# One bank rotation for scores and gradients in the attention core of a fused backward kernel

## The chip, the core and the metric

The kernel runs on one core of a Trainium2 chip. The metric is the device time of one execution in microseconds (us). A core has five engines with a queue of instructions each: TensorE (PE, matrix products, into PSUM banks), VectorE (DVE), ScalarE (ACT), GpSimd (POOL) and SyncE (SP, which here issues transfers). They wait for each other on semaphores, and each runs its own queue in order.

## The reference

Two attention blocks, A and B, read inputs of 2048 tokens with 448 features; the forward output and the gradients of all eight inputs are computed. Block A is linear attention and is untouched here. Block B has 16 heads of width 28 that share one key and one value head:

```
q = (x @ wq) per head;  k = x @ wk;  v = x @ wv
p = softmax(q k^T * 28 ** -0.5);  o = p v;  out = concat(o) @ wo
_out, _vjp = jax.vjp(forward, all inputs);  grads = _vjp(grad_out)
```

Its backward pass needs, for every pair of query and key, the exponential of the score, and the gradient of the probability (the row of "do" against v, less a row term) multiplied with it.

## The kernel before, in words

A prologue computes block A with its gradients and the projections of block B. Then comes the core, one loop over `u`. The queries are cut into 64 blocks `b` (256 query tokens of two heads), and each block into eight steps of 256 keys: `u = 8 b + tp`, 512 steps. The scores of step `u` and the gradients of step `w = u - 16` are computed in one pass of the loop, so that gradients run two blocks behind scores. The order of every engine's queue is the order of the program text (`tc.manual_schedule`).

Eight PSUM banks of 512 words for 128 partitions are in use: three in `SB` (named aacc in the profile), two in `DB` (agen), `oq` and `dk_acc` (agen), and `dv_acc` (aacc). One pass of the loop does, in this order:

- `rows_SD` (its matmuls have the line of `mmt`, L664): eight matmuls of 256 columns, two halves for each of four results: the scores of two heads (sp[0], sp[1]) and the gradients of two heads (dp[0], dp[1]). The tuple (k, h) in `todo` means score (k=0) or gradient (k=1) of head h. The list gives their order in TensorE's queue.
- In even steps `o_dq`, the products for o and dq into `oq`. Then, each once in eight steps and always in even steps, work that uses a bank called `spare`: `onat_T` at u mod 8 = 2, `don_T` at 6, `out_proj` or `do_proj` at 0.
- ScalarE: exponential of sp[0] into `eT` (L935); copy of dp[1] into `cp` (L951); at the end of the pass exponential of sp[1] (L983).
- VectorE: `dst[0] = dp[0] * eT[0]` (L949). POOL: `dst[1] = cp * eT[1]` (L952).
- VectorE's small work, each piece once in eight steps: at u mod 8 = 1 a copy of `oq` (L965), at 2 `o_norm` (L808, L809, which read the spare bank), at 3 L968, at 4 `row_D` (L821, which reads no bank; POOL's L822 behind it), at 6 `don_copy` (L837, reads the spare), at 0 `out_store` (L736) or `do_copy` (L900), which read the spare.
- After the exponentials, each fourth step, SyncE issues a transposing transfer eT to eN.
- In odd steps 16 matmuls `dk_m` that read a transposed block `dsx`; in even steps `o_dq` again and, in three steps out of eight, `dv_mm`.
- In odd steps VectorE transposes the `dsT` pair of the two steps before the last into `dsx` (L1016).

In the kernel before, the scores use the three banks of `SB`, in an order that repeats every four steps, and the one left over is the spare. The gradients use the two banks of `DB`, always the same: dp[0] is DB[0] and dp[1] is DB[1].

Of the kernel before, what the change touches and what calls it, by code (L numbers as in the profile page):

```python
# [8 lines left out]
ACT = mybir.ActivationFunctionType  # L9
# [16 lines left out]
def kernel(  # L26
# [21 lines left out]
    nc = tc.nc  # L48
# [3 lines left out]
    scale = float(DH) ** -0.5  # L52
# [550 lines left out]
    def q_shift(pn, shift, tmp):  # L603
        a = tmp[0][0:H, :]
        nc.scalar.activation(out=a, in_=pn[0:H, :], func=ACT.Identity, bias=eps[:, 0:1], scale=kmax2[:, 0:1])
        i32 = mybir.dt.int32
        nc.vector.tensor_scalar(out=a.bitcast(i32), in0=a.bitcast(i32), scalar1=1, scalar2=None, op0=ALU.logical_shift_right)
        nc.vector.tensor_scalar(out=shift, in0=a, scalar1=1.004 * 2.0 ** 63.5, scalar2=None, op0=ALU.mult)
# [22 lines left out]
    with ExitStack() as cs_:  # L631
# [9 lines left out]
        SB = [psA.tile([P, 512], F32, name="aacc") for i in range(3)]  # L641
        DB = [psA.tile([P, 512], F32, name="agen") for i in range(2)]
        oq, dk_acc = (psA.tile([P, 512], F32, name="agen") for _ in range(2))

        dsT, dsx, qX, don, doT, rl, prod, pairs = ({} for _ in range(8))
        ETs = [pe_.tile([P, 4, 2, 512], BF16, name=f"eT{i}") for i in range(5)]
        ENs = [pn_.tile([P, 32, P], BF16, name=f"eN{i}") for i in range(5)]

        def eT(u):
            return ETs[u // 4 % 5][:, u % 4, :, :]  # L650
# [3 lines left out]
        def half():  # L654
            if not halves:
                t = pd_.tile([P, 2, 2, 512], BF16, name="dsT")
                halves.extend([t[:, 0, :, :], t[:, 1, :, :]])
            return halves.pop(0)
# [4 lines left out]
        def mmt(out, lhsT, rhs, pos, start, stop):  # L663
            nc.tensor.matmul(out, lhsT=lhsT, rhs=rhs, start=start, stop=stop, tile_position=pos,  # L664
                             skip_group_check=True)

        def blk(b):
            qc, pair = divmod(b, 8)
            return qc, pair, pair // 2, pair % 2

        def rows_SD(u, sp, dp):
            b, tp = divmod(u, 8)
            w = u - 16
            qc, pair, g, hp = blk(b)
            todo = [(0, 0), (0, 1), (1, 0), (1, 1)] * 2
            if sp is not None and dp is not None:
                todo = [(0, 0), (1, 0)] * 2 + [(0, 1), (1, 1)] * 2 if u % 2 else \
                    [(0, 0), (0, 1), (1, 0)] * 2 + [(1, 1)] * 2
            seen = {}
            for d in todo:  # L680
                if (dp if d[0] else sp) is None:
                    continue
                k, h = d
                t2 = seen.get(d, 0)
                seen[d] = 1
                t = 2 * tp + t2
                tc_ = slice(t * P, (t + 1) * P)
                oc = slice(t2 * 256, (t2 + 1) * 256)
                r = 64 * (1 - hp if k else hp) + 32 * h
                if k:  # L690
                    mmt(dp[h][:, oc], vT_rep[r:r + 32, tc_], doT[w // 8][r:r + 32, :], (r, 0), True, True)
                else:
                    mmt(sp[h][:, oc], kT_rep[r:r + 32, tc_], qT_B[g][r:r + 32, qc * 256:(qc + 1) * 256],
                        (r, 0), True, True)
# [149 lines left out]
        def qc_T(st, qc, g):  # L844
            nc.sync.dma_start_transpose(qX[qc].rearrange("p b s c -> p (b s) c")[:, :, g * P:(g + 1) * P],
                                        st.rearrange("p n a j -> p (n a j)"))
# [43 lines left out]
        def do_proj(i, c0, c1, ps):  # L890
            for c in range(4):
                if c1 - c0 == 512:
                    mm(ps[:, :], gbT[:, i, c, :], woTp[:, c, :], start=(c == 0), stop=(c == 3))
                    continue
                for j in range(4):
                    js = slice(32 * j, 32 * j + 32)
                    mmt(ps[js, 0:c1 - c0], gbT[:, i, c, js], woTp[:, c, c0:c1], (0, 32 * j), c == 0, c == 3)
# [6 lines left out]
        with tc.manual_schedule():  # L904
# [8 lines left out]
            for u in range(NU + 28):  # L913
                w = u - 16
                hasS = u < NU
                hasD = 0 <= w < NU
                b0, b1, spare = ((SB[i] for i in ((0, 1, 2), (0, 2, 1), (1, 0, 2), (1, 2, 0))[u % 4]) if hasS else SB)
                sp = [b0, b1] if hasS else None
                dp = DB if hasD else None
                rows_SD(u, sp, dp)  # L920
                if u % 2 == 0:
                    o_dq((u - 2,), (u - 20,))
# [5 lines left out]
                    out_proj(*op, spare)  # L928
                dpj = do_slots.pop(u, None)
                if dpj is not None:  # L930
                    dps_ = DB[u // 2 % 2] if u < 16 else dk_acc if u < 27 else spare
                    do_proj(*dpj, dps_)

                if hasS:
                    nc.scalar.activation(out=eT(u)[:, 0, :], in_=sp[0][:, :], func=ACT.Exp, scale=scale)  # L935
                if u == 1:
                    q_shift(pn3, shifts[3], [half().rearrange("p a b -> p (a b)").bitcast(F32)])
                    halves.clear()
                    dv_acc = psA.tile([P, 512], F32, name="aacc")
# [40 lines left out]
                if dpj is not None:  # L980
                    do_copy(*dpj, dps_)
                if hasS:
                    nc.scalar.activation(out=eT(u)[:, 1, :], in_=sp[1][:, :], func=ACT.Exp, scale=scale)  # L983
                    if u % 4 == 3:
                        nc.sync.dma_start_transpose(ENs[u // 4 % 5][:, :, :],
                                                    ETs[u // 4 % 5][:, :, :, :].rearrange("p a b c -> p (a b c)"))
                    if 0 <= gq < 4 and iq == 1 and u < 448:
                        qc_T(qst, qq, gq)

                if u % 2:  # L990
                    b, i = divmod(u - 27, 8)
# [20 lines left out]
                if 0 <= y < NU and y % 2:  # L1012
                    b, tp = divmod(y, 8)
                    if tp == 1:
                        dsx[b] = px_.tile([P, 8, 2, 2, 256], BF16, name="dsx")
                    nc.vector.transpose(  # L1016
                        out=dsx[b][:, tp - 1:tp + 1, :, :, :].rearrange("p u h t c -> p (u h t c)").bitcast(F32),
                        in_=pairs[y // 2].rearrange("p u h c -> p (u h c)").bitcast(F32))
# [70 lines left out]
        for c in range(4):  # L1089
            r = DC_ROWS[c]  # L1090
            ps = gen(0)
            for st in range(NS):
# [3 lines left out]
                                 func=ACT.Copy)  # L1096
# [35 lines left out]
```

## Time and profile before

| | us |
|---|---|
| median of 3 runs (lowest, highest) | 1097.38 (1096.52, 1098.11) |
| profiled execution, whole | 1095.93 |
| its span | 1094.2 |
| busy in the span: TensorE | 1057.8 |
| VectorE | 886.1 |
| ScalarE | 885.0 |
| GpSimd | 784.3 |

The core runs from about 216 to 1050 us, with both scores and gradients from 238 to 1016 us. The granted TensorE clock is full throughout. In the groups of the profile a row gives line, engine, operation, the tile written and those read, their shapes and how often it ran. In a timeline a row is: start, duration, engine, line, operation, tiles, and in brackets the idle time before it and who ended that. A duration counts from an instruction's start to its last write; the next instruction on the same engine can start a little before it.

### The profile page before, as it was taken

How to read it: one execution, taken by the hardware profiler on the slowest of the kernel's cores; microseconds unless marked ns; L12 is line 12 of the kernel's file. 1: busy time of each engine (PE TensorE's matmuls, PEld its weight loads, DVE VectorE, ACT ScalarE, POOL GpSimd, SP SyncE). 2: the span in 40 equal slices, each digit the busy share in tenths (PEclk: the TensorE clock that was granted, in tenths of full speed). 3: DMA queues.
4: the chain of work that ended last, by engine and by line, in shares of the span. 5: the costliest groups of instructions: out<-in, count | busy, mean ns of one | idle time of the engine just before them, and what ended most of it. 6: DMA issues, size and time to landing. Idle time of an engine off the chain costs nothing.

```text
span 1094.2 us, 38903 instructions
## 1 busy us (share of the span) xinstructions
PE 1057.8 (97%) x16241; PEld 470.6 (43%) x16241; DVE 886.1 (81%) x1541; ACT 885.0 (81%) x1741; POOL 784.3 (72%) x1033
## 2 busy tenths in 40 slices
PE   9999999998999999999999999999999999999998
PEld 5555545433444444444434444444444444444334
DVE  7896400668999999999999999999999999999842
ACT  6453122588999999999999999999999999999622
POOL 6001252237988898898889888988988898888882
PEclk9999999999999999999999999999999999999999
DMA  9759898099998999999999999999999999999963
GB/s 268 152 124 190 178 199 212 15 170 191 187 197 164 174 198 180 188 180 197 176 174 190 192 190 173 191 187 174 185 194 183 187 191 189 189 169 178 222 138 92
DMA packets 689928, 195.07 MB, mean 178 GB/s; under 512 B 670616, under 2 KB 687792, under 8 KB 689752
## 3 DMA queue, kind: packets, MB, share of 16 engines
q1 hardware_dynamic: 680152, 179.92, 94.8%
q0 software_dynamic: 4640, 8.71, 2.7%
q10 hardware_dynamic: 4960, 3.96, 1.3%
q8 instruction: 127, 2.08, 0.7%
q14 instruction: 49, 0.40, 0.2%
HBM read 12.60 MB, written 10.84 MB: 21 GB/s over the span
## 4 chain that ended last, share of the span: by engine, by line
PE 74%; DVE 19%; ACT 3%; issue 2%; POOL 1%; DMA 1%; DVEq 0%; ACTq 0%
PE agen L664 34%; PE aacc L664 15%; PE agen L81 14%; DVE dsT L949 8%; DVE dsx L1016 8%; PE aacc L81 7%; DVE R L968 2%; PE aacc L799 1%; ACT cp L951 1%; POOL dsT L952 1%; ACT eT L983 1%; ACT eT L935 1%; DMA dsx<-R 1%; PE aacc L85 0%; PE aacc L830 0%
## 5 line engine op out<-in xcount | busy, mean ns | idle before, releaser
L952 POOL TENSOR_TENSOR dsT<-cp,eT 128x512 bf16<-128x512 bf16 x512 | 589.9, 1157 | 109.4 <-ACT cp L951 101.4
L949 DVE TENSOR_TENSOR dsT<-agen,eT 128x512 bf16<-128x512 f32 x512 | 346.0, 676 | 57.2 <-PE agen L664 45.7
L664 PEld LDWEIGHTS <-R 32*128 32x128 bf16 (+1 forms) x9104 | 211.4, 94 | 353.9 <-issue 331.1
L935 ACT ACTIVATE eT<-aacc 128x512 bf16<-128x512 f32 x512 | 314.7, 615 | 30.0 <-PE aacc L664 15.4
L951 ACT ACTIVATE cp<-agen 128x512 bf16<-128x512 f32 x512 | 315.4, 616 | 13.0 <-PE agen L664 12.3
L983 ACT ACTIVATE eT<-aacc 128x512 bf16<-128x512 f32 x512 | 320.6, 626 | 0.0
L1016 DVE STREAM_TRANSPOSE dsx<-dsT 128x1024 f32<-128x1024 f32 x256 | 315.5, 1233 | 1.0
L664 PE MATMUL aacc<-R,R 32*128 32x256 bf16 (+1 forms) x2240 | 298.4, 268 | 4.1 <-ACT eT L935 0.8
L664 PE MATMUL agen<-doT,R 32*128 32x256 bf16 x2048 | 272.2, 270 | 22.9 <-DVE dsT L949 21.8
L664 PE MATMUL agen<-dsx,qX 32*32 32x512 bf16 x4096 | 268.0, 375 | 0.1
L664 PE MATMUL agen<-eT,R 128*32 128x256 bf16 x2048 | 181.5, 276 | 0.1
L664 PE MATMUL agen<-dsT,R 128*32 128x256 bf16 x2048 | 181.1, 276 | 0.0
L664 PEld LDWEIGHTS <-qX 32*32 32x32 bf16 x4096 | 80.0, 89 | 115.5 <-issue 55.3
L664 PE MATMUL aacc<-eN,don 128*32 128x512 bf16 x1024 | 97.3, 379 | 0.0
L81 PEld LDWEIGHTS <-R 128*128 128x128 bf16 (+1 forms) x517 | 40.8, 98 | 42.6 <-issue 10.6
L406 POOL COPY pk<-R 128x256 bf16<-128x256 bf16 x4 | 1.6, 398 | 73.3 <-DVE R L366 73.2
L81 PE MATMUL agen<-R,R 128*128 128x448 bf16 (+1 forms) x180 | 42.1, 361 | 0.5 <-ACT R L225 0.5
L813 POOL TENSOR_TENSOR prod<-R,oTs 128x128 f32<-128x128 bf16 x64 | 27.6, 432 | 10.0 <-DVE oTs L809 10.0
L664 PEld LDWEIGHTS <-don 128*32 128x32 bf16 x1024 | 34.0, 97 | 0.9
L841 POOL COPY qst<-R 128x512 bf16<-128x512 bf16 x56 | 34.2, 611 | 0.0
L422 DVE TENSOR_TENSOR osb<-aacc,pr 64x448 bf16<-64x448 f32 x2 | 1.2, 616 | 38.0 <-DMA out_dram<-osb 24.0
L968 DVE TENSOR_SCALAR R<-agen 64x256 bf16<-64x256 f32 x64 | 27.3, 426 | 2.0
(231 smaller groups left out, 966.1 us busy)
## 6 DMA issues: line engine op xcount, KB each, us to landing
out_dram<-osb ACTq DMA_DIRECT2D x22, 112.0 KB
eN<-eT SPq DMA_TRANSPOSE x128
xa<-in_A_x_dram SPq DMA_DIRECT2D x8, 224.0 KB
ga<-in_grad_out_dram SPq DMA_DIRECT2D x4, 448.0 KB
xa<-in_grad_out_dram POOLq DMA_DIRECT2D x4, 448.0 KB, 5.9
out_dram<-wdq POOLq DMA_DIRECT2D x8, 224.0 KB, 4.3
eT<-in_grad_out_dram SPq DMA_DIRECT2D x4, 448.0 KB
eT<-in_B_x_dram SPq DMA_DIRECT2D x4, 448.0 KB
```

The source lines that it names most:

```text
L81: nc.tensor.matmul(out_ap, lhsT=lhsT, rhs=rhs, start=start, stop=stop, tile_position=(0, 0))
L664: nc.tensor.matmul(out, lhsT=lhsT, rhs=rhs, start=start, stop=stop, tile_position=pos, skip_group_check=True)
L799: nc.tensor.transpose(onp[:, qb, :, :].rearrange("p h c -> p (h c)"), oTs[0:64, qb * P:(qb + 1) * P], identF[0:64, 0:64], tile_position=(0 ...
L813: nc.gpsimd.tensor_tensor(out=prod[b][:], in0=dnv, in1=os_, op=ALU.mult)
L841: eng.tensor_copy(out=st.rearrange("p (b s) a j -> p b s a j", s=2)[:, :, s, :, :], in_=src.unsqueeze(2).to_broadcast([P, 4, 4, 32]))
L935: nc.scalar.activation(out=eT(u)[:, 0, :], in_=sp[0][:, :], func=ACT.Exp, scale=scale)
L949: nc.vector.tensor_tensor(out=dst[:, 0, :], in0=dp[0][:, :], in1=ew[:, 0, :], op=ALU.mult)
L951: nc.scalar.activation(out=cp[:, :], in_=dp[1][:, :], func=ACT.Copy)
L952: nc.gpsimd.tensor_tensor(out=dst[:, 1, :], in0=cp[:, :], in1=ew[:, 1, :], op=ALU.mult)
L968: nc.vector.tensor_scalar(out=qT_B[g][64 * hp:64 * hp + 64, qc * 256:(qc + 1) * 256], in0=oq[64:128, 0:256], scalar1=scale, scalar2=None, ...
L983: nc.scalar.activation(out=eT(u)[:, 1, :], in_=sp[1][:, :], func=ACT.Exp, scale=scale)
L1016: nc.vector.transpose(out=dsx[b][:, tp - 1:tp + 1, :, :, :].rearrange("p u h t c -> p (u h t c)").bitcast(F32), in_=pairs[y // 2].rearrang ...
```

## The change

The three score banks and the two gradient banks become one list of five, `RB`. The roles move over the banks from step to step: `banks[u]` names the banks of the first score, the first gradient, the second score, the second gradient and the spare. From an even step to the odd one after it the first score keeps its bank, the first gradient takes the spare, the second score takes the first gradient's bank, the second gradient the second score's, and the second gradient's becomes the spare. From an odd step to the even one the first score takes the spare, the first gradient the first score's bank, and the other three move as before. The orders of `rows_SD` change with it: in odd steps the first gradient is computed last, in even steps all four take turns. The second exponential moves ahead of the gradient copy on ScalarE. In the first 16 steps `do_proj` uses the second gradient's bank.

```diff
+        RB = SB + DB
+        banks = [(0, 3, 1, 4, 2)]
+        while len(banks) < 512:
+            s0, d0, s1, d1, x = banks[-1]
+            banks.append((x, s0, d0, s1, d1) if len(banks) % 2 == 0 else (s0, x, d0, s1, d1))
...
             todo = [(0, 0), (0, 1), (1, 0), (1, 1)] * 2
             if sp is not None and dp is not None:
-                todo = [(0, 0), (1, 0)] * 2 + [(0, 1), (1, 1)] * 2 if u % 2 else \
-                    [(0, 0), (0, 1), (1, 0)] * 2 + [(1, 1)] * 2
+                todo = [(0, 0), (0, 1), (1, 1)] * 2 + [(1, 0)] * 2 if u % 2 else todo
...
-                b0, b1, spare = ((SB[i] for i in ((0, 1, 2), (0, 2, 1), (1, 0, 2), (1, 2, 0))[u % 4]) if hasS else SB)
-                sp = [b0, b1] if hasS else None
-                dp = DB if hasD else None
+                s0, d0, s1, d1, spare = (RB[i] for i in (banks[u] if hasS else (0, 3, 1, 4, 2)))
+                sp = [s0, s1] if hasS else None
+                dp = [d0, d1] if hasD else None
...
-                    dps_ = DB[u // 2 % 2] if u < 16 else dk_acc if u < 27 else spare
+                    dps_ = d1 if u < 16 else dk_acc if u < 27 else spare
...
                     nc.scalar.activation(out=eT(u)[:, 0, :], in_=sp[0][:, :], func=ACT.Exp, scale=scale)
+                    nc.scalar.activation(out=eT(u)[:, 1, :], in_=sp[1][:, :], func=ACT.Exp, scale=scale)
...
-                    nc.scalar.activation(out=eT(u)[:, 1, :], in_=sp[1][:, :], func=ACT.Exp, scale=scale)
                     if u % 4 == 3:
                         nc.sync.dma_start_transpose(ENs[u // 4 % 5][:, :, :],
```

## The prediction

> **What bounds the kernel now.** I read the busy shares first, then the waits between 300 and 1040 us (the long middle, where one loop repeats), then the timelines of VectorE and TensorE over one group of eight steps. I write u for the step and "u=1" for u mod 8 = 1; S0, S1 are the two score banks of a step, D0, D1 its two gradient banks; "multiply" is L949, "transpose" is L1016.
>
> ```profile
> PE 1057.8 (97%) x16241; PEld 470.6 (43%) x16241; DVE 886.1 (81%) x1541; ACT 885.0 (81%) x1741; POOL 784.3 (72%) x1033
> ```
>
> These shares average the middle with a long prologue, and PE's 97% counts overlapping matmuls, so they name no bound. The waits of the middle say more (us in total, times, longest):
>
> ```profile
> POOL dsT L952 <- ACT cp L951: 87.3, 252, 0.7
> DVE dsT L949 <- PE agen L664: 40.9, 143, 1.2
> PE agen L664 <- DVE dsT L949: 16.8, 60, 0.9
> ```
>
> VectorE's multiply waits for TensorE's D matmuls, and those wait for VectorE's multiply: a loop through one bank, D0. VectorE's timeline over a pair of steps, u=7 and 0, up to u=1, shows it (start, length):
>
> ```profile
> 604.40 0.69 DVE L949 TENSOR_TENSOR dsT<-agen,eT 128x512 bf16<-128x512 f32 x1 [0.28 <-PE agen L664]
> 605.01 1.23 DVE L1016 STREAM_TRANSPOSE dsx<-dsT 128x1024 f32<-128x1024 f32 x1
> 606.17 0.65 DVE L949 TENSOR_TENSOR dsT<-agen,eT 128x512 bf16<-128x512 f32 x1
> 606.74 0.26 DVE L736 CAST ot<-aacc 128x112 bf16<-128x112 f32 x1
> 607.28 0.69 DVE L949 TENSOR_TENSOR dsT<-agen,eT 128x512 bf16<-128x512 f32 x1 [0.28 <-PE agen L664]
> ```
>
> The only idle time is 0.28 before the odd multiply. Call t0 the end of the even multiply, here 606.17 + 0.65 = 606.82. TensorE at that place:
>
> ```profile
> 606.57 0.28 PE L664 MATMUL aacc<-R,R 32*128 32x256 bf16 x1
> 606.87 0.27 PE L664 MATMUL agen<-doT,R 32*128 32x256 bf16 x1
> 606.88 0.28 PE L664 MATMUL aacc<-R,R 32*128 32x256 bf16 x1
> 606.98 0.27 PE L664 MATMUL agen<-doT,R 32*128 32x256 bf16 x1
> 607.05 0.26 PE L664 MATMUL aacc<-R,R 32*128 32x256 bf16 x1
> ```
>
> PE arrives at 606.57, does S0's first half, and stands until t0 + 0.05. Then D0's halves start at 606.87 and 606.98; the second ends 0.27 later and the multiply starts 0.03 after that: t0 + 0.46. Small VectorE work of the even step (here the 0.26 cast) lies in that 0.46 and costs nothing. S1, at 607.05, is what waits for the cast (it reuses the spare bank), off the loop. At u=2 and u=4 the small work is longer or other:
>
> ```profile
> 609.38 0.65 DVE L949 TENSOR_TENSOR dsT<-agen,eT 128x512 bf16<-128x512 f32 x1
> 609.95 0.16 DVE L808 RECIPROCAL rl<-aacc 128x4 f32<-128x4 f32 x1
> 610.15 0.29 DVE L809 TENSOR_TENSOR oTs<-aacc,rl 128x128 f32<-128x128 f32 x1
> 610.49 0.69 DVE L949 TENSOR_TENSOR dsT<-agen,eT 128x512 bf16<-128x512 f32 x1
> ```
>
> ```profile
> 612.82 0.69 DVE L949 TENSOR_TENSOR dsT<-agen,eT 128x512 bf16<-128x512 f32 x1
> 613.43 0.28 DVE L821 TENSOR_REDUCE Dq<-prod 128x4 f32<-128x128 f32 x1
> 613.98 0.69 DVE L949 TENSOR_TENSOR dsT<-agen,eT 128x512 bf16<-128x512 f32 x1 [0.27 <-PE agen L664]
> ```
>
> Again t0 + 0.46 and t0 + 0.47. From 604.40 to 607.28 the loop is 0.61 + 1.16 + 0.65 + 0.46 = 2.88 per pair; the odd steps' oTs copy and L968 lengthen two pairs in four. The same L968 stands at 598.63 and 611.21: 12.58 per eight steps, 62 such groups where scores and gradients both run (u 16 to 511). ScalarE starts an operation each 0.48 (602.40, 602.87, 603.35): 24 of them are 11.5 of the 12.58, close behind.
>
> **The change, part by part.** Following the tuples, in every odd step S1 takes the bank that was D0 in the even step, D0 takes the even step's spare, D1 the even S1, and S0 keeps its bank. In even steps S0 takes the spare, D0 the old S0, S1 the old D0, D1 the old S1. Nothing is added or removed on any engine; waits move.
>
> *Odd step, matmuls.* S1 is now first to wait for t0, and it is second in PE's queue; D0, now last of the eight, stands behind it. So D0 starts no earlier than before, though its own bank may be free. The working, from t0: S1's first half at +0.05, with D1's and S0's waiting ones beside it; the second halves 0.11 to 0.12 later (the step between 606.87 and 606.98), at +0.17; D0's first half 0.01 behind (in the even step at 605.48 the four banks' second halves start at 605.60 and 605.61), at +0.18; its second at +0.29, ended at +0.56, multiply at +0.59. Against 0.46 this is **+0.13**, in every odd step at least.
>
> *Odd step, the spare.* D0 now also waits for whoever last read the even step's spare, and that is VectorE's small work, queued behind the even multiply. It was covered by the refill; now the refill (0.05 + 0.11 + 0.27 + 0.03 = 0.46) begins after it.
> - u=1: cast ends 607.00, multiply at 607.46 instead of 607.28: **+0.18**.
> - u=3: L809 ends 610.44, multiply at 610.90 instead of 610.49: **+0.41**.
> - u=5: the reduce reads no bank, the spare is unused: **+0.13** from the order alone.
> - u=7: the doT copy at 603.86 lasts 0.26 and ends 604.12; 604.58 instead of 604.40: **+0.18**.
>
> Sum 0.90 per eight steps, times 62: 55.8. In 11 groups (L736 at 128x224: 7 and 4) the cast is 0.39 long: at 1020.93 it ends 1021.32, so 1021.78 instead of 1021.39, 0.21 more than counted, 2.3 in all. Together 58.1.
>
> *What is behind the longer wait.* PE's dk matmuls (16, 607.38 to 608.4) start behind the last of the eight: D0's second half at t0 + 0.29 to 0.34 at u=1 (now 607.18, t0 + 0.36) and at 610.60 at u=3 (now 610.62). They move by nothing, so the even step's D0 is there on time, before the transpose ends.
>
> *Even step.* All four banks go round at once; S1 waits for the odd multiply, D0 for exp 0. Exp 0 of the odd step can start at t0 + 0.37 and ends by t0 + 0.97; the odd multiply ends by t0 + 1.3 (u=3: 1.6); PE is in dk until about t0 + 1.5 (1.75). Cover 0.15 to 0.5, so nothing. Without it, D0 would still have until the transpose ends, about t0 + 2.4.
>
> *Exponentials ahead of the copy.* Same 1024 + 512 operations. The copy, and POOL's L952 behind it, come 0.48 later in the step. The transpose at 602.13 (u=5) reads POOL's product of u=3, the first of the two that run from 599.71 for 2.27, so ended near 600.9: over 1 us of cover, 0.48 of it goes. Tightest is POOL's L822, queued behind L952 at u=4: it ended at 602.15, PE's don transposes that read it ran at 603.10: 0.95, of which 0.48 goes. I take nothing; if that cover were gone, up to 0.4 per group, 25 in all. The exponentials' early end frees S banks for D banks, which no wait of the loop asks for. SyncE's eN transposes are issued up to 0.48 sooner, in the same order; their data is read over ten steps later: nothing.
>
> *Steps 0 to 15.* do_proj uses D1's bank; VectorE's copies are the same. ScalarE idles 0.22 before L935 in about seven of these steps: between -2 and +0.5, I take 0.
>
> **A rule against the trace.** The 0.27 to 0.28 hole comes back before three of four odd multiplies. The Trainium skill (Perfetto Trace Analysis, Optimization Strategy) says that a gap repeating on an engine that should be saturated can mean too little PSUM for the next tile. By that rule, pooling five banks should close the hole: the gain of the rival below. The rows agree with the reading of the hole but not with this cure: the bank count is the same, and the matmul that stands first on the even multiply has only changed its name from D0 to S1.
>
> **The rivals.**
> *Faster.* D0 refills in the spare while the even multiply still runs, and the holes at u=1, 5 and 7 (0.28 + 0.27 + 0.28) go: 0.83 x 62 = 51, to 1046. It needs PE to reach S1 after t0. PE is there at 606.57 against 606.82, at 613.11 against 613.51: 0.25 to 0.4 early, and a longer loop makes it earlier. The faster outcome decides from the point where that lead is below zero. 3%.
> *No change.* ScalarE's 11.5 per group were the true bound and VectorE's holes only follow it: 1097. But ScalarE itself idles 0.29 before the exponential at 601.43. 2%.
> *Less.* The spare's readers do not bite (u=3 above all) and only the order does: 0.13 x 4 x 62 = 32, 1130 or below. 7%.
> *More.* POOL's delay reaches PE at the don transposes or ScalarE falls behind: 25 on top, 1180 or above. 7%.
>
> **How the numbers follow.** The profiled execution took 1095.93 (span 1094.2 and 1.7 around it); the median is 1.45 above. 1095.93 + 58.1 = 1154.0, as a median 1155.5: I say 1155, with 81% for this mechanism at about this size. The range runs from the "less" case to the "more" case, 1130 to 1180. Both signs within 0.2%, about what a measurement of this kernel can tell from no change, count as same: faster 0.03, same 0.02, slower 0.95.
>
> **What would show it.** After the change, VectorE's time per eight steps is near 13.5 instead of 12.58; idle time before L949 released by PE roughly doubles, with 0.38 to 0.46 between the small work's end and the odd multiply; at u=3 the multiply starts 0.46 after L809 instead of 0.05. PE's S1 in odd steps starts 0.05 after the even multiply and D0 after it. ScalarE's busy time is unchanged. Wrong would be: D0's matmuls ahead of t0, or idle before L949 below 40 us, or new waits at POOL's L822 that outweigh the rest.

## The result, and the profile after

The change makes the kernel slower: 1157.53 us median (1157.04 to 1160.56) against 1096.95 for the kernel before in the same runs, a ratio of 1.0557 with a 95% interval of [1.0536, 1.0578]. The profiled execution took 1157.27 us, 61.3 above the 1095.93 of before.

The page's first line, and the waits from 300 to 1040 us, in the order of the lines shown of before:

```profile
PE 1064.3 (92%) x16232; PEld 466.2 (40%) x16241; DVE 885.4 (77%) x1541; ACT 897.5 (78%) x1741; POOL 786.8 (68%) x1033
```

```profile
POOL dsT L959 <- ACT cp L958: 133.1, 307, 0.9
DVE dsT L956 <- PE aacc L671: 99.6, 219, 0.6
...
PE agen L671 <- DVE dsT L956: 38.3, 103, 0.7
...
PE aacc L671 <- DVE dsT L956: 19.5, 54, 0.7
```

VectorE does the same work (885.4 us, before 886.1). Its multiply (now L956) waits for TensorE 99.6 us where it waited 40.9, and TensorE waits for the multiply 57.8 where it waited 16.8. The loop that the prediction named has grown. Other waits grew with it: POOL's for the copy from 87.3 to 133.1 us, ScalarE's first exponential's for TensorE from 8.6 to 59.1. The intervals given below the table show that none of them lengthens the time from an odd multiply to the even one after it. VectorE's timeline from u=4 to u=3 of the next group:

```profile
641.33 0.69 DVE L956 TENSOR_TENSOR dsT<-agen,eT 128x512 bf16<-128x512 f32 x1
641.94 0.28 DVE L827 TENSOR_REDUCE Dq<-prod 128x4 f32<-128x128 f32 x1
642.63 0.69 DVE L956 TENSOR_TENSOR dsT<-aacc,eT 128x512 bf16<-128x512 f32 x1 [0.42 <-PE aacc L671]
...
644.40 0.65 DVE L956 TENSOR_TENSOR dsT<-aacc,eT 128x512 bf16<-128x512 f32 x1
645.08 0.29 DVE L843 COPY doT<-aacc 64x256 bf16<-64x256 bf16 x1
645.84 0.69 DVE L956 TENSOR_TENSOR dsT<-aacc,eT 128x512 bf16<-128x512 f32 x1 [0.46 <-PE aacc L671]
...
651.12 0.64 DVE L956 TENSOR_TENSOR dsT<-agen,eT 128x512 bf16<-128x512 f32 x1
651.70 0.16 DVE L814 RECIPROCAL rl<-aacc 128x4 f32<-128x4 f32 x1
651.89 0.29 DVE L815 TENSOR_TENSOR oTs<-aacc,rl 128x128 f32<-128x128 f32 x1
652.64 0.69 DVE L956 TENSOR_TENSOR dsT<-aacc,eT 128x512 bf16<-128x512 f32 x1 [0.46 <-PE aacc L671]
```

Where the small work reads the spare (u=6 and u=2 here) the idle 0.46 now begins at its end; before, the small work lay inside the refill. For all the runs I took, from the starts of the multiplies in the trace, the mean time from an even multiply to the odd one after it, by the odd step, and the sum of a group of eight steps (59 groups from u=40 on):

| kernel (us) | u=1 | u=3 | u=5 | u=7 | group | u=16 starts at | median |
|---|---|---|---|---|---|---|---|
| before | 1.12 | 1.14 | 1.16 | 1.12 | 12.56 | 238.3 | 1096.95 |
| changed | 1.32 | 1.52 | 1.30 | 1.37 | 13.54 | 239.6 | 1157.53 |
| x1: D0 ahead of S1 | 1.29 | 1.52 | 0.80 | 1.42 | 13.10 | 239.4 | 1131.24 |
| x2: spare to D1 | 1.30 | 1.22 | 1.26 | 1.22 | 13.03 | 242.7 | 1128.97 |
| x3: copy second | 1.97 | 1.80 | 1.57 | 1.96 | 15.58 | 239.4 | 1282.89 |
| x8: tiny read | 1.32 | 1.52 | 1.23 | 1.38 | 13.47 | 239.4 | 1154.16 |
| x10: D0 keeps its bank | 1.14 | 1.12 | 1.16 | 1.12 | 12.55 | 243.4 | 1100.77 |
| x4: before, copy last | 1.36 | 1.42 | 1.16 | 1.41 | 13.37 | 238.0 | 1146.77 |
| x5: D0 in exp 0's bank | 1.25 | 1.01 | 0.94 | 1.30 | 12.54 | 244.4 | 1101.63 |
| x6: same, D0 first | 1.12 | 1.30 | 0.80 | 1.21 | 12.58 | 240.8 | 1099.80 |
| x9: same, copy second | 1.15 | 1.29 | 0.80 | 1.24 | 12.59 | 238.7 | 1099.08 |
| x11: before, spare at u=5 | 1.15 | 1.21 | 0.80 | 1.16 | 12.33 | 238.7 | 1083.32 |

The four odd-to-even intervals are 8.02 together before and after the change. So the loss is 0.985 per group, all of it before the odd multiplies. From the multiply of step 16 to that of step 512, 62 groups, the changed kernel takes 59.8 us longer (782.0 before, 841.8 after). Another 1.3 us are lost ahead of step 16 (239.6 against 238.3): together 61.1 of the 61.3.

### The profile page after: what moved, and what is told of

Read it like the earlier page. It is cut to its first block, busy times and chain, and to the rows that moved or that the text cites. A ratio compares the mean times of both kernels' runs of the same rounds, so it can differ in the third digit from the quotient of the medians.

```text
span 1155.6 us, 39608 instructions
## 1 busy us (share of the span) xinstructions
PE 1064.3 (92%) x16232; PEld 466.2 (40%) x16241; DVE 885.4 (77%) x1541; ACT 897.5 (78%) x1741; POOL 786.8 (68%) x1033
## 4 chain that ended last, share of the span: by engine, by line
PE 62%; DVE 23%; issue 11%; ACT 3%; DMA 1%; DVEq 0%; ACTq 0%
PE agen L671 28%; DVE dsT L956 16%; PE agen L81 13%; PE aacc L671 10%; PE aacc L81 7%; DVE dsx L1022 5%; ACT eT L942 2%; PE aacc L805 2%; DVE R L975 1%; DMA dsx<-R 1%; PE aacc L85 0%; PE aacc L836 0%; PE agen L223 0%; PE agen L364 0%; DVE pq L240 0%
## 5 line engine op out<-in xcount | busy, mean ns | idle before, releaser
L956 DVE TENSOR_TENSOR dsT<-aacc,eT 128x512 bf16<-128x512 f32 x330 | 225.7, 684 | 113.8 <-PE aacc L671 113.2
L671 PE MATMUL agen<-R,R 32*128 32x256 bf16 x1022 | 202.0, 272 | 49.9 <-DVE dsT L956 44.2
L941 ACT ACTIVATE eT<-agen 128x512 bf16<-128x512 f32 x340 | 203.5, 599 | 52.1 <-PE agen L671 43.2
L671 PE MATMUL aacc<-doT,R 32*128 32x256 bf16 x1322 | 209.7, 270 | 1.4
L671 PE MATMUL aacc<-R,R 32*128 32x256 bf16 (+1 forms) x1218 | 186.4, 265 | 26.5 <-DVE dsT L956 23.0
L942 ACT ACTIVATE eT<-aacc 128x512 bf16<-128x512 f32 x341 | 202.5, 594 | 0.0
L958 ACT ACTIVATE cp<-aacc 128x512 bf16<-128x512 f32 x331 | 199.9, 604 | 0.0
L956 DVE TENSOR_TENSOR dsT<-agen,eT 128x512 bf16<-128x512 f32 x182 | 120.4, 662 | 4.8 <-PE agen L671 3.4
L941 ACT ACTIVATE eT<-aacc 128x512 bf16<-128x512 f32 x172 | 103.0, 599 | 26.1 <-PE aacc L671 20.1
L958 ACT ACTIVATE cp<-agen 128x512 bf16<-128x512 f32 x181 | 109.7, 606 | 13.1 <-PE agen L671 12.4
L671 PE MATMUL agen<-doT,R 32*128 32x256 bf16 x726 | 106.5, 272 | 2.0 <-DVE dsT L956 2.0
L942 ACT ACTIVATE eT<-agen 128x512 bf16<-128x512 f32 x171 | 101.1, 591 | 0.0
```

What stands on the lines that cost most here:

```text
L956: nc.vector.tensor_tensor(out=dst[:, 0, :], in0=dp[0][:, :], in1=ew[:, 0, :], op=ALU.mult)
L958: nc.scalar.activation(out=cp[:, :], in_=dp[1][:, :], func=ACT.Copy)
```

## The experiments

The diffs are against the changed kernel, save x4, x9 and x11, which start from the kernel before. They show the lines that carry the change; in x5, x6 and x9 the replaced lines are left out.

**x1: the order term alone.**

```diff
-                todo = [(0, 0), (0, 1), (1, 1)] * 2 + [(1, 0)] * 2 if u % 2 else todo
+                todo = [(0, 0), (1, 0)] * 2 + [(0, 1), (1, 1)] * 2 if u % 2 else todo
```

> The changed kernel with the odd steps' old order: first gradient D0 ahead of the second score S1, bank rotation kept. My theory (two terms: D0 stands behind S1, which waits for the even multiply; and D0 waits for the spare bank's VectorE reader): the order term goes, the spare term stays. From the start of the even multiply to that of the odd one: 1.29 at u=1, 1.52 at u=3, 1.30 at u=7 as in the changed kernel, but only about 0.90 at u=5, where the spare is unused (1.30 now). Some 0.4 to 0.5 per eight steps, times 62: 25 to 31 us less than the changed kernel's 1157, about 1128. Rival (the cost is the spare's readers alone, order does not matter): 1157. Rival (the cost is the late copy on ScalarE): 1157, with u=5 unchanged.

Measured: 1131.24 (ratio to before 1.0313, [1.0296, 1.0331]). Only u=5 falls, from 1.30 to 0.80, as expected; the other three keep theirs within 0.05, since D0 waits there for the spare's reader whatever its place in the queue. VectorE at u=4 and 5 now runs without a hole:

```profile
628.42 0.69 DVE L956 TENSOR_TENSOR dsT<-agen,eT 128x512 bf16<-128x512 f32 x1
629.02 0.28 DVE L827 TENSOR_REDUCE Dq<-prod 128x4 f32<-128x128 f32 x1
629.22 0.68 DVE L956 TENSOR_TENSOR dsT<-aacc,eT 128x512 bf16<-128x512 f32 x1
```

**x2: the spare taken off D0.**

```diff
-            banks.append((x, s0, d0, s1, d1) if len(banks) % 2 == 0 else (s0, x, d0, s1, d1))
+            banks.append((x, s0, d0, s1, d1) if len(banks) % 2 == 0 else (s0, s1, d0, x, d1))
...
-                todo = [(0, 0), (0, 1), (1, 1)] * 2 + [(1, 0)] * 2 if u % 2 else todo
+                todo = [(0, 0), (0, 1), (1, 0)] * 2 + [(1, 1)] * 2 if u % 2 else todo
```

> The changed kernel with two roles swapped in odd steps: the first gradient D0 takes the second score's old bank (free after its exponential), the second gradient D1 takes the spare; odd order (S0, S1, D0) twice, then D1 twice. D0 still comes after S1's wait for the even multiply, but inside the same round, and no longer waits for the spare's reader. My theory: even to odd multiply is 1.10 to 1.17 in all four pairs, as before the change, so about 1097 to 1103. Rival (sharing five banks or the late copy costs by itself): 1140 or more.

Measured: 1128.97 (1.0292, [1.0277, 1.0308]). A partial miss. The spare's part goes where it was largest (u=3 from 1.52 to 1.22, u=7 from 1.37 to 1.22), but no pair returns to 1.12. At u=3, 5 and 7, 0.08 to 0.10 stays. The multiply's line has 499 wait instructions in x2 and 318 in the changed kernel: here every odd multiply has a second wait, and in the pair at 640 us (u=3) it starts 0.107 after D0's last matmul, against 0.038 where it has none. x8 takes up this wait. At u=1 D0's new bank is freed by the second exponential, which is late too: in the pair at 714 us it ends at 715.02 and D0 starts at 715.07. The first 16 steps also lost 3 us to the new roles.

**x3: ScalarE's order undone.** The second exponential goes back to the end of the pass; the rest is the changed kernel.

> The changed kernel with only ScalarE's order undone: exponential 0, copy, exponential 1. If the late copy were the cause of the loss (rival), 1097 to 1130. My theory says that the copy's place cost nothing in the changed kernel, and that with the rotation the order is even needed: D1 of the odd step takes S1's even bank, and exponential 1 then ends 0.48 later, after the even multiply, with D0 queued behind D1: 1157 at the least, up to 0.25 more per pair, 1157 to 1220.

Measured: 1282.89 (1.1696, [1.1677, 1.1716]), 125 above the changed kernel, where I had allowed 63 at most. The rival is out: putting the copy back does not undo the loss. In the changed kernel the early second exponential saves the rotation. TensorE in x3, from u=6 to u=7:

```profile
642.76 0.28 PE L671 MATMUL aacc<-R,R 32*128 32x256 bf16 x1
642.76 0.28 PE L671 MATMUL agen<-R,R 32*128 32x256 bf16 x1
643.52 0.26 PE L671 MATMUL aacc<-doT,R 32*128 32x256 bf16 x1 [0.48 <-ACT eT L989]
```

S0's and S1's first halves start at 642.76, and D1 holds the whole queue, their second halves too, until 643.52, when the late exponential lets go of its bank; D0 is behind it.

**x4: ScalarE's order alone, on the kernel before.** Both exponentials ahead of the copy.

> The kernel before with ScalarE's order alone changed: both exponentials ahead of the gradient copy; banks and matmul orders as before. D1 then has one bank whose copy ends 0.48 later: in odd steps D1 waits for it to about 0.45 after the even multiply, in even steps for that of the odd step, and the products behind D1 in PE's queue come later. My theory: not free, 20 to 90 us more than before, so 1117 to 1187; the reorder needs the rotation, as the rotation needs the reorder. Rival (the copy's place is hidden anyway): 1097 to 1100.

Measured: 1146.77 (1.0457, [1.0443, 1.0471]): within the wide range of my theory. In the pair at 724 us (u=3) TensorE begins the odd step's matmuls at 725.33, 0.30 after the even multiply's end at 725.03, where it stood ready before that end in the kernel before; and D1 starts at 725.74, 0.04 after its copy let go of the bank. ScalarE's order without the rotation costs 50 us against the kernel before; the rotation without the order, in x3, costs 125 against the changed kernel.

**x8: one column read by VectorE.**

```diff
+        scr = pw_.tile([P, 1], F32, name="scr", bufs=1)
...
                     nc.vector.tensor_tensor(out=dst[:, 0, :], in0=dp[0][:, :], in1=ew[:, 0, :], op=ALU.mult)
+                    if u % 8 == 4 and hasS:
+                        nc.vector.tensor_copy(out=scr[:, :], in_=spare[:, 0:1])
```

> The changed kernel with one more VectorE instruction in each step with u mod 8 = 4: a copy of one column of the spare bank to a scratch tile, right after the even multiply. In the trace of the changed kernel the odd multiply at u=5 has a second wait instruction ahead of it, for ScalarE, and starts 0.15 after the last gradient matmul instead of 0.04; at u=1, 3 and 7, where VectorE was the last reader of the bank before, it has none. My theory: that second wait comes because ScalarE was the bank's last reader, and it costs 0.11 per eight steps. With the read, VectorE is the last reader: even to odd 1.19 instead of 1.30 at u=5, 62 x 0.11 = 7 us less than the changed kernel, about 1150. Rival (the 0.61 at u=5 is the order of the matmuls, as I predicted): no change, 1157, or slightly more.

Measured: 1154.16 (1.0522, [1.0507, 1.0536]), 3.4 less than the changed kernel's median; its profiled execution 1153.03, 4.2 less. In the instructions of the multiply's line, the wait instructions of the kernel before, the changed kernel and x8 are:

```profile
L949 DVEq EVENT_SEMAPHORE  x2: 50/50/50, 244.1 to 248.0; - x2
```

```profile
L956 DVEq EVENT_SEMAPHORE  x318: 21/21/315, 239.5 to 1080.9; - x159
```

```profile
L957 DVEq EVENT_SEMAPHORE  x256: 21/21/315, 239.3 to 1076.6; - x128
```

The one-column read, which adds an instruction, takes away exactly 62 waits, one per group. At u=5 the odd multiply then starts 0.05 after the last gradient matmul instead of 0.15; the read delays the matmul by 0.03, so 0.07 per group is left, 0.07 x 62 = 4.3. The mechanism is shown; its size was about half of the 7 us that I expected.

**x10: the roles of before on five shared banks.**

```diff
-            banks.append((x, s0, d0, s1, d1) if len(banks) % 2 == 0 else (s0, x, d0, s1, d1))
+            banks.append((x, s0, d0, s1, d1) if len(banks) % 2 == 0 else (s0, d0, x, s1, d1))
...
-                todo = [(0, 0), (0, 1), (1, 1)] * 2 + [(1, 0)] * 2 if u % 2 else todo
+                todo = [(0, 0), (1, 0)] * 2 + [(0, 1), (1, 1)] * 2 if u % 2 else todo
```

> The changed kernel with five shared banks, even steps and ScalarE's order as they are, but in odd steps D0 keeps the even D0's bank and S1 takes the spare (the kernel before's roles), with the odd order of the kernel before. My theory: sharing the banks and copying last cost nothing by themselves, only what D0 of the odd step waits for does; even to odd multiply back to 1.11 to 1.16 in all four pairs, no second wait ahead of the odd multiply, 12.5 to 12.65 per eight steps, 1094 to 1104. Rival (part of the loss is in the sharing or in ScalarE's order): 1110 or more.

Measured: 1100.77 (1.0033, [1.0020, 1.0045]). A group takes 12.55, as before the change. The 4 us that remain are in the first 16 steps: the multiply of step 16 starts at 243.4 instead of 238.3. So with these roles neither pooling the banks nor the place of the copy costs anything in the loop; what the odd D0 and S1 wait for, and their order, is the whole loss there.

**x5, x6 and x9: closing the hole everywhere.** x5 gives the odd D0 the bank of the even S0, S0 that of the even S1, S1 that of the even D0, D1 the spare. x6 also puts both halves of D0 first and leaves steps 0 to 15 as in the kernel before. x9 does the same with ScalarE's old order.

```diff
# x5
+            banks.append((x, s0, d0, s1, d1) if len(banks) % 2 == 0 else (s1, s0, d0, x, d1))
+                todo = [(1, 0), (0, 0)] * 2 + [(0, 1), (1, 1)] * 2 if u % 2 else todo
# x6, instead of x5's todo
+                todo = [(1, 0)] * 2 + [(0, 0), (0, 1)] * 2 + [(1, 1)] * 2 if u % 2 else todo
# x9, as x6, and
+            banks.append((x, s0, d0, d1, s1) if len(banks) % 2 == 0 else (d1, s0, d0, x, s1))
```

> The changed kernel with another rotation in odd steps: D0 takes the bank of the even S0 (free after exponential 0, well ahead of the end of the even multiply), S0 that of the even S1, S1 that of the even D0, D1 the spare; odd order D0, S0 twice, then S1, D1 twice. If my reading of the loop is right, the hole before the odd multiply goes altogether: even to odd 0.85 at u=1, 1.10 at u=3, 0.88 at u=5, 0.87 at u=7, so 11.7 per eight steps on VectorE, with ScalarE's 24 operations of 0.48 = 11.5 just below: 11.7 to 12.1 against 12.55, times 62, 28 to 53 us less than the kernel before: 1044 to 1070. Rival (ScalarE or PE was the true bound of the kernel before, and the hole only follows it): 1097 or within a few us of it.

> The rotation of the run with D0 in the exponential 0 bank, with both halves of D0 first in odd steps (its second half stood behind S0, which waits for exponential 1), and with the banks of the kernel before in the first 16 steps (that run lost about 6 us there). My theory: the hole before the odd multiply goes in all four pairs (even to odd 0.85 to 0.95 at u=1, 5, 7, 1.10 or less at u=3, VectorE 11.7 per eight steps); ScalarE then sets the pace: S0 waits for exponential 1 of the even step, which leaves ScalarE 0.13 idle per pair, 4 x (6 x 0.48 + 0.13) = 12.1. 12.1 to 12.3 against 12.55: 16 to 28 us less than before, 1069 to 1081. Rival (PE, whose matmuls fill about 11.4 of the 12.55, takes over): 1090 or more.

> As the run before it in this call, but with ScalarE's old order (exponential 0, copy, exponential 1) and banks to suit: in odd steps D0 takes the bank of exponential 0, S0 that of the copy, S1 that of the even D0, D1 the spare. ScalarE's idle time per pair 0.10, 12.0 to 12.3 per eight steps: 1063 to 1081. Rival (PE takes over): 1090 or more.

Measured: 1101.63, 1099.80 and 1099.08 (1.0033 [1.0018, 1.0048], 1.0025 [1.0015, 1.0035] and 1.0020 [1.0011, 1.0029]). My expectation failed, all three times; the rival held. The hole at u=5 closes in x6 and x9 (0.80), and the group still takes 12.58 and 12.59. TensorE, VectorE and ScalarE of x6 from u=0 to u=1:

```profile
646.93 0.60 ACT L945 ACTIVATE eT<-aacc 128x512 bf16<-128x512 f32 x1
...
647.17 0.39 PE L671 MATMUL aacc<-doT,R 32*128 32x256 bf16 x2
647.18 0.27 DVE L742 CAST R<-aacc 128x112 bf16<-128x112 f32 x1
...
647.59 0.26 PE L671 MATMUL aacc<-R,R 32*128 32x256 bf16 x1
647.59 0.28 PE L671 MATMUL agen<-R,R 32*128 32x256 bf16 x1
...
647.66 0.69 DVE L959 TENSOR_TENSOR dsT<-aacc,eT 128x512 bf16<-128x512 f32 x1 [0.21 <-PE aacc L671]
```

D0 is no longer held by anyone: it starts at 647.17 because TensorE only gets there then, with the cast already running. And S0 now stands until the second exponential, 646.93 + 0.60, has ended. My reading is that with these roles a loop through TensorE and ScalarE is as long as the one through VectorE's hole was; it rests on this pair, and no run isolates it. The profile's chain of x6 from 300 to 1040 us lies on TensorE's matmuls for 70% and on ScalarE for 3%, so TensorE alone may set the pace, as the rival had it. That stays open.

**x11: the hole closed in one place.** The kernel before, with only steps u=5 changed: D0 takes the spare that nobody uses at u=4, S1 the even D0's bank.

```diff
+            n = len(banks)
+            banks.append((x, d0, s0, d1, s1) if n % 2 == 0 else
+                         (s0, x, d0, d1, s1) if n % 8 == 5 and n > 16 else (s0, d0, x, d1, s1))
```

> The kernel before (its matmul orders, ScalarE's order and first 16 steps) with one change: in steps with u mod 8 = 5, whose even neighbour leaves the spare unused, D0 takes the spare and S1 takes the even D0's bank; all other steps keep the roles of the kernel before. My theory: the hole ahead of the multiply at u=5 closes (even to odd 0.80 instead of 1.155), 0.35 per eight steps, of which the loop through PE and ScalarE (3.0 per pair where the hole was closed everywhere) gives back part in the next pair: 0.15 to 0.30 net, times 62: 9 to 19 us less than before, 1078 to 1088. Rival (PE and ScalarE are as close as VectorE, and the next pair gives back all of it): 1094 to 1099.

Measured: 1083.32 (0.9882, [0.9865, 0.9898]): 1.2% faster than the kernel before, with the interval clear of 1. Of the 0.35 that u=5 gains, the pairs at u=7, 1 and 3 give back 0.05, 0.03 and 0.07, and the odd-to-even intervals are 0.01 shorter: 0.22 net per group (12.555 to 12.333), 0.22 x 62 = 13.8 against 13.3 measured.

```profile
643.72 0.69 DVE L957 TENSOR_TENSOR dsT<-agen,eT 128x512 bf16<-128x512 f32 x1
644.33 0.28 DVE L829 TENSOR_REDUCE Dq<-prod 128x4 f32<-128x128 f32 x1
644.52 0.68 DVE L957 TENSOR_TENSOR dsT<-aacc,eT 128x512 bf16<-128x512 f32 x1
```

## Why the prediction was right, point by point

*The bound and the sum.* The loop through the odd D0 was the right place: all of the loss lies before odd multiplies. Per group I summed 0.90, and 0.04 more on average for the wide casts; measured 0.985. The total for the loop, 58.1, stands against 59.8. That it came so near is luck in part: the terms below miss by -0.03 to +0.08, and those of u=7 and u=5 for reasons that I did not have.

*u=3, +0.41.* Measured medians 1.11 and 1.52: +0.41 (+0.38 in the mean), and the idle 0.46 after L815 as written. x2, which takes the spare away from D0, gives 0.30 of it back.

*u=1, +0.18 and +0.39 where the cast is wide.* Measured +0.18 at the median and +0.20 in the mean, which holds the wide ones.

*u=7, +0.18.* Mis-sized: +0.26. I read the doT copy's end from one step of the trace, at 0.19 after the even multiply. In the same trace it ends at 0.19 in every second group and at 0.32 in the others, where the copy starts only 0.03 after the multiply's end; the mean is 0.26. It was inside the hole and did not show. In the changed kernel it does: 645.08 + 0.29 is 0.32 after 645.05, the multiply's end.

*u=5, +0.13.* The number was near (+0.15) and the reason wrong. I had D0's first half queue behind the second halves of S1 and D1. TensorE at that place:

```profile
642.08 0.26 PE L671 MATMUL agen<-R,R 32*128 32x256 bf16 x1 [0.61 <-DVE dsT L956]
642.08 0.28 PE L671 MATMUL aacc<-doT,R 32*128 32x256 bf16 x1
642.08 0.28 PE L671 MATMUL aacc<-R,R 32*128 32x256 bf16 x1
642.09 0.28 PE L671 MATMUL aacc<-doT,R 32*128 32x256 bf16 x1
642.18 0.27 PE L671 MATMUL agen<-R,R 32*128 32x256 bf16 x1
642.20 0.28 PE L671 MATMUL aacc<-doT,R 32*128 32x256 bf16 x2
```

The second gradient matmul, at 642.09, is D0's first half: it starts 0.09 before S1's second half, which is ahead of it in the queue but whose rows are still busy. The order cost about 0.03. The other 0.11 was a second wait instruction on VectorE that I had not seen coming (x8).

*The rule on repeated gaps.* The hole did not close, as the row had said. x10 shows the same pooled banks at 12.55 per group with the old roles, so the count of banks was not the matter. x11 closes one of the holes by a bank that stood unused, with the count unchanged: there the hole did come from the lack of a free bank for D0.

*ScalarE, POOL and SyncE at nothing.* Right in the time: the loss is all before odd multiplies, and x10 has ScalarE's new order and no loss in the loop. Two readings beside it were wrong. I wrote that no wait of the loop asks for the early end of the second exponential; x3 shows that the rotation does, with 125 us. And I wrote that ScalarE's busy time is unchanged; it is 897.5 us against 885.0 with the same 1741 instructions, whose lengths add up to less than before (1029.7 against 1060.6 us). So they overlap less, and the busy time counts an overlap once. The rival "no change" counted on ScalarE setting the pace; it is not the first bound of the kernel before, as x11 shows. x6 and x9 show that something else stands close behind it, ScalarE or TensorE. *The faster rival* needed TensorE to reach S1 after the even multiply; TensorE waited for the multiply 57.8 us instead of 16.8.

*Steps 0 to 15 at nothing.* Mis-sized: the multiply of step 16 starts 1.3 us later than before. x9 and x11, which use the banks of the kernel before in these steps, have it at 238.7, x6, with those banks and ScalarE's new order, at 240.8, x10 at 243.4; no run isolates what costs the time.

## What to carry to other kernels

When PSUM banks change roles, write down for each matmul the last reader of its bank, and where that reader stands in its own engine's queue: small work queued behind a long instruction is free in a hole; once a refill waits for it, it costs the time by which it outlasts the long one (0.41 us at u=3, 0.18 at u=1). A bank that stands unused in some steps is worth most there, and the gain is taken only as far as the next loop allows: closing one hole of four gave 13 us, going after all four at once, with the roles of x5, x6 and x9, gave nothing.

## What the runs showed of the hardware

- An instruction that has to wait for two engines gets a wait instruction of its own ahead of it. On VectorE, at u=5, the multiply then starts 0.151 after the last matmul it needs, against 0.038 in the kernel before. The Trainium skill (Perfetto Trace Analysis, Identifying Dependency Chains) says that such instructions may be inserted; the trace agrees, and it gives the price, 0.11. They appeared here where the previous reader of D0's bank was ScalarE, and 62 of them went when a read by VectorE came between (x8). x10, where only the even D0 has such a bank, has 250 on the multiply's line, x2, where every D0 has one, 499. Ahead of the even multiplies they cost nothing that shows: the odd-to-even intervals stay at 8.02.
- TensorE's queue is held whole by a matmul that waits for a semaphore (x3: 0.48), but a matmul that only waits for busy rows lets a later one start on idle rows, 0.09 ahead (642.09 against 642.18, by the starts in the trace, with the order of the queue taken from the program text). The Trainium skill (TensorEngine Tiling (Array Packing), Key Properties) says that different tiles can work in parallel; the trace agrees, and shows that this holds against the order of the queue too.
